# Attention's exponential images: one of four moved from VectorE to GpSimd, in three batches of four

## The chip, the core and the metric

The kernel runs on one core of one Trainium2 chip. The metric is the device time of one execution in microseconds (us). The core has five engines that run side by side and wait for each other by semaphores. The profile's names for them are PE (TensorE, matrix products into PSUM), DVE (VectorE), ACT (ScalarE), POOL (GpSimd) and SP (SyncE, which only issues DMAs here); PEld is PE's loading of weights.

## What is computed

Four layers over x of 2048 rows and 512 columns in bfloat16: a spectral layer A, an attention layer B, then both again with the same weights. Each adds its result to x.

```python
x = x + A(layernorm(x))        # rfft2, times W, irfft2
x = x + B(layernorm(x))
x = x + A(layernorm(x))
x = x + B(layernorm(x))

def B(x):                      # 32 heads of 16, one shared key and value head
    q = (x @ wq).reshape(2048, 32, 16)
    k, v = x @ wk, x @ wv
    scores = einsum("qhd,kd->hqk", q, k) * 16 ** -0.5
    return einsum("hqk,kd->qhd", softmax(scores), v).reshape(2048, 512) @ wo
```

The change lies in B, apart from one small table.

## The kernel before

**Groups and steps.** An attention layer (attention_layer, L529) works through 32 groups: 4 blocks of 512 queries times 8 sets of 4 heads. A group has 64 score tiles of 128 keys by 512 queries, 16 key chunks (kc) times 4 heads (h). Three quarters of them, those with h != kc % 4, get their exponential on ACT, three tiles at a time: one such triple is a step, so a group has 16 steps (the first group of a layer has 18, for its first four key chunks go to ACT altogether). `s0[g]` is the first step of group g.

**The other quarter goes to DVE**, as integer arithmetic. For one tile a step, `t_new` (L725) turns the scores in PSUM into 16-bit integers, steps of a logarithm. Four such tiles, from four key chunks, are a batch b (four batches a group, one per four steps). From each batch four images (L731, `s_new`, 128x2048) are made with different offsets (PH_OFF): read as bfloat16, an image is a piecewise linear exponential, and the sum of the four with weights PH_W smooths the error out. So DVE makes one t_new and one image in every step, the image one to four steps behind the last t_new of its batch.

**PE** makes the scores: `dv` (L601, one tile in a PSUM tile of its own with one buffer) for DVE and `sc` (L601, three tiles, two buffers) for ACT. It then multiplies with the values (`pv_new`, L713): four matmuls for an image and three for a triple of exponentials, all summed in one PSUM tile of the group. The values' matrix has the weights of the images in it and a column of ones, whose sum is the softmax denominator.

**The order of the work** is written out by hand. The loop at L734 walks the steps n; `chain` (L541) ties each engine's instructions to the order in which the loop issued them. In a step come, in this order: work that was put off (`later`), the eviction of a finished group, dve_step (dv, t_new, image), act_step (sc, exponential e), then pv_step with the matmuls of two steps earlier (LAG = 2). PE thus queues dv of a step, then sc, then the matmuls, and an earlier one that waits holds up the later ones.

**A group's boundary.** Two steps into the next group `evict` (L614) copies the finished sum from PSUM (`o`, L616); in the same step, in place of pv_step, PE projects the queries of the group after next (L459) into the PSUM buffer that o has left. One step later `qevict` (L462) casts them to `qt` (L464) and clears half of the rows with a bitwise AND against a table (L465). Only then can the matmuls of the new group start, for they use the same PSUM buffer; those of two steps are made together. The denominators go to DRAM and back, are inverted (L624), and are spread to all rows by DMA (`rb`, L629).

**POOL** multiplies o with rb (L657), in three cuts of 176, 176 and 160 columns in three steps (12 to 14 of the group). `pace` (L605) makes each cut wait for the latest image on DVE.

**A layer's end.** After the last step the output projection is made in PSUM triples (L767 on, `triple`), and each 128x512 result is added to x by `finish` (L682): with `with_x` PE adds x by an identity matmul and ACT casts (L685), without it DVE adds x (L687). In the first attention layer, two of a triple go to ACT and one to DVE (`n_x`, L764); statistics and normalisation of the next layer's input run between them. In the last layer all of these go to DVE, and the last four results (three in one PSUM triple, one by itself) go to ACT, except the second.

Of the kernel before, what the change touches and what calls it, by code (L numbers as in the profile page):

```python
# [10 lines left out]
ALU = mybir.AluOpType  # L11
P = 128
BF = mybir.dt.bfloat16
# [4 lines left out]
NT = 16  # L18
NC = 4
R = 4  # L20
T = 4
# [5 lines left out]
I16 = mybir.dt.int16  # L27
# [11 lines left out]
T_MUL = SCALE * LOG2E * 256.0  # L39
# [3 lines left out]
def host_tables():  # L43
    import ml_dtypes
    bf = lambda a: np.ascontiguousarray(np.asarray(a, dtype=np.float32).astype(ml_dtypes.bfloat16))
    f32 = lambda a: np.ascontiguousarray(np.asarray(a, dtype=np.float32))
    w0 = 2 * np.pi / 2048.0
    tabs = {}

    sp = (128 * np.arange(4)[None, None, :, None] + np.arange(P)[:, None, None, None]).astype(np.float64)  # L50
    tt = np.arange(4)[None, :, None, None].astype(np.float64)
    k1 = np.arange(256)[None, None, None, :].astype(np.float64)
    ang = w0 * k1 * (4 * sp + tt)
    alt = np.broadcast_to(1.0 - 2.0 * (sp % 2), ang.shape[:3] + (1,))
# [36 lines left out]
    tabs["KAB"] = f32(np.stack([1.0 - half, -THETA * half], axis=1))  # L91
    tabs["QAND"] = np.ascontiguousarray(np.broadcast_to(np.where(half == 0, -1, 0x7FFF).astype(np.int16)[:, None], (P, 512)))
    tabs["ident"] = bf(eye)
    return tabs

# [350 lines left out]
def attention_inputs(nc, tabs, shared, xn_sb, aw):  # L446
# [15 lines left out]
    def qevict(ps):  # L462
        qt = shared.tile([P, 512], BF, tag="QT", bufs=3)
        nc.vector.tensor_copy(out=qt, in_=ps)  # L464
        nc.vector.tensor_tensor(out=qt.bitcast(I16), in0=qt.bitcast(I16), in1=tabs["QAND"], op=ALU.bitwise_and)  # L465
        return qt

    def filler(psum, rhs, n):
# [60 lines left out]
def attention_layer(nc, tc, tabs, shared, lnpool, x_sb, xn_sb, aw, prep, nxt, store):  # L529
    with ExitStack() as ctx:  # L530
# [26 lines left out]
        act_tiles = []  # L557
        for g in range(NG):
            s0[g] = len(act_tiles)
            us = [(g, kc, h) for kc in range(NT) for h in range(4)  # L560
                  if h != kc % 4 or (g == 0 and kc < 4)]
            act_tiles += [us[i:i + 3] for i in range(0, len(us), 3)]
        s0[NG] = len(act_tiles)
        d_score, d_phase = {}, {}
        for g in range(NG):
            for kc in range(NT):
                if not (g == 0 and kc < 4):
                    d_score[s0[g] + kc - 4] = (g, kc)
                    if g == 0:
                        base = 4 + (kc // 4 - 1) * 4  # L570
                    else:
                        base = s0[g] + kc - kc % 4
                    d_phase[base + kc % 4] = (g, kc // 4, kc % 4)
        LAG = 2
        first_pv, last_pv = {}, {}
        pv_list = {}
        evict_at = {s0[g + 1] + LAG: g for g in range(NG)}
        qproj_at = {s0[g + 1] + LAG: g + 2 for g in range(NG - 2)}
        for n0 in range(s0[NG]):
            lst = []  # L580
            if n0 in d_phase:
                g, b, j = d_phase[n0]
                lst += [(g, 4 * b + i, i, j, n0) for i in range(4)]
            lst += [(g, kc, h, -1, n0) for (g, kc, h) in act_tiles[n0]]
            assert len({u[0] for u in lst}) == 1
            n = n0 + LAG
            if n in evict_at:
                n += 1
            pv_list.setdefault(n, []).extend(lst)
            for u in lst:  # L590
                first_pv.setdefault((u[0], u[2]), u)
                last_pv[(u[0], u[2])] = u

        psc = ctx.enter_context(tc.tile_pool(name="psc", bufs=2, space=bass.MemoryType.PSUM))
        psd = ctx.enter_context(tc.tile_pool(name="psd", bufs=1, space=bass.MemoryType.PSUM))
# [3 lines left out]
        def score(dst, g, kc, h):  # L599
            hs = slice(32 * h, 32 * h + 32)  # L600
            nc.tensor.matmul(dst, lhsT=KT[hs, kc * P:(kc + 1) * P], rhs=QT[g][hs, :], start=True, stop=True)  # L601
# [87 lines left out]
                store(r, t, nc.sync if t == T - 1 and r % 2 == 1 else nc.gpsimd)  # L689

        chain()
        def act_step(n):
# [8 lines left out]
            nc.scalar.activation(out=e[:, 0:na, :], in_=sc[:, 0:na, :], func=ACT.Exp, scale=SCALE)  # L701

        def pv_step(n):
            for u in pv_list.get(n, ()):
                g, kc, h, j, n0 = u
                if g not in pv:
                    pv_new = psp.tile([P, 512], F32, tag="pv")
                    pv[g] = pv_new
                if j < 0:
                    rhs = ex[n0][:, act_tiles[n0].index((g, kc, h)), :]  # L710
                else:
                    rhs = sb[(g, kc // 4, j)][:, h, :].bitcast(BF)
                nc.tensor.matmul(pv[g][32 * h:32 * h + 32, :], lhsT=vaug[:, max(j, 0), kc, :], rhs=rhs,  # L713
                                 start=(g > 0 and first_pv[(g, h)] == u), stop=(last_pv[(g, h)] == u),
                                 skip_group_check=True)

        def dve_step(n):
            if n in d_score:
                g, kc = d_score[n]
                dv = psd.tile([P, 512], F32, tag="dv")  # L720
                score(dv, g, kc, kc % 4)
                if kc % 4 == 0:
                    t_new = work.tile([P, 4, 512], I16, tag="T", bufs=3)
                    tb[(g, kc // 4)] = t_new
                nc.vector.tensor_scalar(out=tb[(g, kc // 4)][:, kc % 4, :], in0=dv, scalar1=T_MUL, scalar2=T_ADD,  # L725
                                        op0=ALU.mult, op1=ALU.add)
            if n in d_phase:
                g, b, j = d_phase[n]
                s_new = work.tile([P, 4, 512], I16, tag="S", bufs=7)
                sb[(g, b, j)] = s_new  # L730
                image[0] = nc.vector.tensor_scalar(out=s_new, in0=tb[(g, b)], scalar1=0.5, scalar2=16384.0 + PH_OFF[j],  # L731
                                                   op0=ALU.mult, op1=ALU.add)

        for n in range(s0[NG]):  # L734
            now[0] = n
# [25 lines left out]
            chain()  # L761


        mv, n_x = {}, 0 if nxt is None else 2  # L764

        def triple(i):
            ps = psc.tile([P, 3, 512], F32, tag="sc", name="tri")  # L767
# [249 lines left out]
```

## Time and profile before

| | us |
|---|---|
| runs | 1647.89, 1647.89, 1650.95 |
| median | 1647.89 |
| the profiled execution | 1655.24 |
| its span, first to last instruction | 1653.4 |
| first attention layer, loop of steps | 119 to 813 |
| second attention layer, loop of steps | 935 to 1630 |
| busy: PE, DVE, ACT, POOL | 1428.4, 1551.4, 1509.0, 163.2 |

The profiled execution is one run with the hardware profiler on. Its times count from the first instruction, and its span is compared with its own 1655.24, not with the median. A row of a group gives the line, the engine, the operation, what it writes and reads, shapes and count, then busy time and the mean duration of one in ns, then idle time before it and what ended that. A row of the timeline gives start and length in us; consecutive instructions of one kind may be merged into one row with a count. Neighbouring instructions of one engine overlap in the record: while DVE is never idle, a t_new of 685 ns is followed by the next operation 0.60 us after its start. The clock granted to TensorE was 0.943 over the span.

### The profile page before, as it was taken

Reading aid. Unit: us, or ns where it says so; the run is one execution under the profiler, and the core shown is the slowest. Engines: PE = TensorE matmul, PEld = TensorE weight load, DVE = VectorE, ACT = ScalarE, POOL = GpSimd, SP = SyncE. Lnnn points to the kernel's source line nnn. Section 1 sums busy time; section 2 is a strip of 40 time slices with the busy share of each in tenths; the row PEclk is TensorE's granted clock in tenths of the full one; section 3 lists DMA queues with packets and bytes.
Section 4 is the critical chain, followed back from the end, with each engine's and each line's share of the span. In section 5 each row is a group of like instructions: output and inputs, shape, how many; then the busy total and the mean of one; then the engine's idle time right before and its main releaser. Section 6 shows DMA issues by size and latency. Waiting matters only on the chain.

```text
span 1653.4 us, 32260 instructions
## 1 busy us (share of the span) xinstructions
PE 1428.4 (86%) x12768; PEld 461.3 (28%) x12768; DVE 1551.4 (94%) x2793; ACT 1509.0 (91%) x1254; POOL 163.2 (10%) x277
## 2 busy tenths in 40 slices
PE   6798888888888888888988988888888888888887
PEld 2342222222222222222333322222222222222222
DVE  6979999999999999999778799999999999999995
ACT  5369999999999999999853799999999999999994
POOL 3210000000000000000102000000000000000002
PEclk9899999999999999999998999999999999999999
DMA  8000000000000010001020000000000000000002
GB/s 289 5 1 8 17 17 17 17 16 11 16 17 17 16 30 16 16 17 30 23 71 0 1 9 16 17 17 17 17 17 17 17 17 17 12 15 17 16 17 66
DMA packets 46536, 40.78 MB, mean 25 GB/s; under 512 B 30832, under 2 KB 34416, under 8 KB 46000
## 3 DMA queue, kind: packets, MB, share of 16 engines
q1 hardware_dynamic: 45712, 36.88, 7.9%
q8 instruction: 100, 1.64, 0.4%
q0 software_dynamic: 672, 1.84, 0.3%
q14 instruction: 52, 0.43, 0.1%
HBM read 33.57 MB, written 3.15 MB: 22 GB/s over the span
## 4 chain that ended last, share of the span: by engine, by line
ACT 32%; DVE 29%; issue 21%; PE 16%; POOL 1%; DMA 1%; SPq 0%; DVEq 0%; POOLq 0%; ACTq 0%
ACT e L701 31%; DVE t_new L725 11%; DVE s_new L731 9%; PE pv_new L713 4%; PE fd L268 2%; PE dv L601 2%; DVE o L616 2%; DVE qt L464 2%; PE sc L601 2%; DVE qt L465 1%; DVE stats L125 1%; PE tri L679 1%; PE ps L391 1%; PE ps L379 1%; PE ps L192 1%
## 5 line engine op out<-in xcount | busy, mean ns | idle before, releaser
L701 ACT ACTIVATE e<-sc 128x1536 bf16<-128x1536 f32 (+1 forms) x1028 | 1387.5, 1532 | 6.2 <-PE sc L601 5.8
L725 DVE TENSOR_SCALAR t_new<-dv 128x512 int16<-128x512 f32 x1016 | 695.5, 685 | 26.4 <-PE dv L601 8.9
L731 DVE TENSOR_SCALAR s_new<-t_new 128x2048 int16<-128x2048 int16 x1016 | 698.6, 689 | 0.0
L601 PE MATMUL dv<-qt,KT 32*128 32x512 bf16 x1016 | 384.1, 378 | 108.1 <-DVE t_new L725 106.0
L601 PE MATMUL sc<-qt,KT 32*128 32x512 bf16 x3080 | 409.0, 383 | 33.9 <-ACT e L701 4.3
L713 PE MATMUL pv_new<-s_new,vaug 128*32 128x512 bf16 x4064 | 410.4, 391 | 27.2 <-DVE qt L464 27.2
L713 PE MATMUL pv_new<-e,vaug 128*32 128x512 bf16 x3080 | 412.9, 390 | 0.3 <-ACT e L701 0.3
L601 PEld LDWEIGHTS <-KT 32*128 32x128 bf16 x4096 | 201.2, 91 | 721.4 <-issue 702.8
L713 PEld LDWEIGHTS <-vaug 128*32 128x32 bf16 x7144 | 135.3, 94 | 265.7 <-issue 251.2
L657 POOL TENSOR_TENSOR ot_new<-o,rb 128x176 bf16<-128x176 f32 (+1 forms) x96 | 55.0, 575 | 700.0 <-DVE s_new L731 649.3
L657 POOL TENSOR_TENSOR od<-o,rb 128x176 bf16<-128x176 f32 (+1 forms) x90 | 49.4, 549 | 598.7 <-DVE s_new L731 598.7
L459 PE MATMUL ps<-xT,wq_sb 128*128 128x512 bf16 x256 | 67.3, 387 | 11.4 <-DVE o L616 11.4
L379 PE MATMUL ps<-tab_PS,st 128*128 128x512 bf16 x128 | 36.1, 448 | 16.2 <-DVE st L327 12.7
L385 ACT CAST U<-ps 128x512 bf16<-128x512 f32 x24 | 14.0, 585 | 36.4 <-PE ps L379 36.4
L268 PE MATMUL fd<-X,tab_DT 128*128 128x512 bf16 x192 | 43.9, 390 | 2.7 <-DVE X L242 2.7
L274 ACT CAST xn_sb<-fd 128x512 bf16<-128x512 f32 x32 | 18.7, 585 | 28.5 <-PE fd L268 28.5
L464 DVE CAST qt<-ps 128x512 bf16<-128x512 f32 x64 | 44.2, 691 | 0.4 <-PE ps L459 0.4
L616 DVE COPY o<-pv_new 128x512 f32<-128x512 f32 x64 | 43.8, 685 | 0.2 <-PE dv L601 0.2
L125 DVE BATCH_NORM_STATS2 stats<-x_sb 128x6 f32<-128x512 bf16 x46 | 30.7, 676 | 7.2 <-DMA x_sb<-in_A_x_dram 3.5
L459 PEld LDWEIGHTS <-wq_sb 128*128 128x128 bf16 x256 | 25.0, 97 | 40.2 <-issue 16.6
L391 PE MATMUL ps<-U,IT 128*128 128x512 bf16 x128 | 34.3, 390 | 0.0
L192 PE MATMUL ps<-FT,xn_sb 128*128 128x512 bf16 x80 | 22.2, 439 | 13.9 <-ACT xn_sb L134 10.9
(154 smaller groups left out, 602.1 us busy)
## 6 DMA issues: line engine op xcount, KB each, us to landing
rb<-d SPq DMA_DIRECT2D x256, 64.0 KB
FT<-const_FT SPq DMA_DIRECT2D x8, 512.0 KB
IT<-const_IT SPq DMA_DIRECT2D x8, 512.0 KB
x_sb<-in_A_x_dram SPq DMA_DIRECT2D x4, 512.0 KB
ot_new<-od SPq DMA_DIRECT2D x120, 16.0 KB
out_dram<-x_sb POOLq DMA_DIRECT2D x14, 128.0 KB, 2.2
tab_DT<-const_DT SPq DMA_DIRECT2D x1, 1280.0 KB
wr_raw<-in_A_w_r_dram SPq DMA_DIRECT2D x1, 1028.0 KB
```

The source lines that it names most:

```text
L268: nc.tensor.matmul(pss[i], lhsT=DT[:, b, w, 128 * fb:128 * fb + 128], rhs=X[:, b, part, c, :, :].rearrange("p k j -> p (k j)"), start=star ...
L379: nc.tensor.matmul(ps, lhsT=st[c][:, t, vec, q, fb, :], rhs=PS[:, fb, w, :], start=(k == 0), stop=(k == 3))
L391: nc.tensor.matmul(ps, lhsT=IT[:, t, part, c, r * P:(r + 1) * P], rhs=U[:, t, part, c, :], start=(k == 0), stop=(k == 3 and r % 2 == 1), s ...
L459: nc.tensor.matmul(ps, lhsT=wq_sb[:, c, hg, :], rhs=xTq[qb][:, c, :], start=(c == 0), stop=(c == NC - 1))
L464: nc.vector.tensor_copy(out=qt, in_=ps)
L601: nc.tensor.matmul(dst, lhsT=KT[hs, kc * P:(kc + 1) * P], rhs=QT[g][hs, :], start=True, stop=True)
L616: nc.vector.tensor_copy(out=o, in_=pv.pop(g))
L657: pace(nc.gpsimd.tensor_tensor(out=dst[:, a:b], in0=o[:, a:b], in1=rb[:, a:b], op=ALU.mult))
L701: nc.scalar.activation(out=e[:, 0:na, :], in_=sc[:, 0:na, :], func=ACT.Exp, scale=SCALE)
L713: nc.tensor.matmul(pv[g][32 * h:32 * h + 32, :], lhsT=vaug[:, max(j, 0), kc, :], rhs=rhs, start=(g > 0 and first_pv[(g, h)] == u), stop=(l ...
L725: nc.vector.tensor_scalar(out=tb[(g, kc // 4)][:, kc % 4, :], in0=dv, scalar1=T_MUL, scalar2=T_ADD, op0=ALU.mult, op1=ALU.add)
L731: image[0] = nc.vector.tensor_scalar(out=s_new, in0=tb[(g, b)], scalar1=0.5, scalar2=16384.0 + PH_OFF[j], op0=ALU.mult, op1=ALU.add)
```

## The change

On POOL, batches 0, 1 and 2 of a group (the first group of a layer has only 1 and 2) get their fourth image, in four pieces of 128x512, one piece per step at steps 4b to 4b + 3, each paced behind the latest image on DVE. DVE makes the other three images of these batches, and all four of batch 3. They lie at steps 0, 4, 5 (batch 0), 6 to 8, 9 to 11 and 12 to 15, so that steps 1, 2 and 3 have none. The matmuls are taken from a queue of lists, at most three lists a step, everything that is left in the step ahead of an eviction, and none in the step of the eviction.

```diff
-    tabs["QAND"] = np.ascontiguousarray(np.broadcast_to(np.where(half == 0, -1, 0x7FFF).astype(np.int16)[:, None], (P, 512)))
+    tabs["QAND"] = np.ascontiguousarray(np.where(half == 0, -1, 0x7FFF).astype(np.int16)[:, None])
...
-        nc.vector.tensor_tensor(out=qt.bitcast(I16), in0=qt.bitcast(I16), in1=tabs["QAND"], op=ALU.bitwise_and)
+        nc.vector.tensor_scalar(out=qt.bitcast(I16), in0=qt.bitcast(I16), scalar1=tabs["QAND"], scalar2=None, op0=ALU.bitwise_and)
...
+                for j, k in enumerate(((0, 4, 5), (6, 7, 8), (9, 10, 11), (12, 13, 14, 15))[b]):
+                    d_image[s0[g] + k] = (g, b, j)
+                if b < 3:
+                    for i in range(4):
+                        p_image[s0[g] + 4 * b + i] = (g, b, i)
...
+        queue = []
+        for n in range(s0[NG] + LAG):
+            n0 = n - LAG
+            if n0 in d_image:
+                g, b, j = d_image[n0]
+                queue.append([(g, kc, h, j, i) for i, (kc, h) in enumerate(batch[(g, b)])])
+            if n0 in p_image and p_image[n0][2] == 3:
+                g, b, _ = p_image[n0]
+                queue.append([(g, kc, h, 3, i) for i, (kc, h) in enumerate(batch[(g, b)])])
+            if 0 <= n0:
+                queue.append([(g, kc, h, -1, (n0, i)) for i, (g, kc, h) in enumerate(act_tiles[n0])])
             if n in evict_at:
-                n += 1
+                continue
+            count = len(queue) if n + 1 in evict_at else min(len(queue), 3)
+            pv_list[n] = sum(queue[:count], [])
+            queue = queue[count:]
...
+        scratch = shared.tile([P, 3, 4, 512], I16, tag="G", bufs=1)
+
+        def steps_of(g, b):
+            k = len(tb)
+            if (g, b) not in tb:
+                tb[(g, b)] = scratch[:, k % 3]
+            return tb[(g, b)]
...
         def dve_step(n):
...
+            if n in d_image:
+                g, b, j = d_image[n]
                 s_new = work.tile([P, 4, 512], I16, tag="S", bufs=7)
                 sb[(g, b, j)] = s_new
-                image[0] = nc.vector.tensor_scalar(out=s_new, in0=tb[(g, b)], scalar1=0.5, scalar2=16384.0 + PH_OFF[j],
-                                                   op0=ALU.mult, op1=ALU.add)
+                image[0] = nc.vector.tensor_scalar(out=s_new, in0=tb[(g, b)], **image_of(j))
+            if n in p_image:
+                g, b, i = p_image[n]
+                if i == 0:
+                    pool_new = work.tile([P, 4, 512], I16, tag="SP", bufs=2)
+                    sb[(g, b, 3)] = pool_new
+                pace(nc.gpsimd.tensor_scalar(out=sb[(g, b, 3)][:, i, :], in0=tb[(g, b)][:, i, :], **image_of(3)))
...
-        mv, n_x = {}, 0 if nxt is None else 2
+        mv, n_x = {}, 0 if nxt is None else 3
...
-            outproj(12 + i, pf[i], i != 1)
+            outproj(12 + i, pf[i], i < 3)
...
-            finish(12 + i, pf[i], i != 1)
+            finish(12 + i, pf[i], i < 3)
```

`image_of(j)` holds the two constants of an image, as before, and `to_steps` the t_new instruction, as before. The integer tiles were three buffers of a tag of their own and are now thirds of `scratch`, which lies in the shared buffer of tag G; that buffer holds the spectral layers' G and U, and is free between them. The AND's table shrinks from 512 columns to one. At the layers' ends, in the first attention layer all three of a triple go to ACT, and in both layers the last four go to ACT for the three of one PSUM triple and to DVE for the one by itself.

More of the change, by code (lines that the diff above doesn't have):

```diff
@@ L559, in attention_layer @@
             s0[g] = len(act_tiles)
-            us = [(g, kc, h) for kc in range(NT) for h in range(4)
-                  if h != kc % 4 or (g == 0 and kc < 4)]
+            us = [(g, kc, h) for kc in range(NT) for h in range(4) if h != kc % 4 or (g == 0 and kc < 4)]
             act_tiles += [us[i:i + 3] for i in range(0, len(us), 3)]
         s0[NG] = len(act_tiles)
-        d_score, d_phase = {}, {}
+        d_score, d_image, p_image, batch = {}, {}, {}, {}
         for g in range(NG):
[L566 to L573, printed above, removed]
+            for b in range(NT // 4):
+                if g == 0 and b == 0:
+                    continue
+                batch[(g, b)] = [(4 * b + i, i) for i in range(4)]
+                for i in range(4):
+                    d_score[s0[g] + 4 * b + i - 4] = (g, b, i)
+                for j, k in enumerate(((0, 4, 5), (6, 7, 8), (9, 10, 11), (12, 13, 14, 15))[b]):
+                    d_image[s0[g] + k] = (g, b, j)
+                if b < 3:
+                    for i in range(4):
+                        p_image[s0[g] + 4 * b + i] = (g, b, i)
@@ L574, in attention_layer @@
         LAG = 2
-        first_pv, last_pv = {}, {}
-        pv_list = {}
+        first_pv, last_pv, pv_list = {}, {}, {}
         evict_at = {s0[g + 1] + LAG: g for g in range(NG)}
         qproj_at = {s0[g + 1] + LAG: g + 2 for g in range(NG - 2)}
[L579 to L586, printed above, removed]
-            if n in evict_at:
-                n += 1
-            pv_list.setdefault(n, []).extend(lst)
-            for u in lst:
+        queue = []
@@ new lines, in attention_layer @@
+        for n in range(s0[NG] + LAG):
[8 more added lines that the diff above has]
+                queue.append([(g, kc, h, -1, (n0, i)) for i, (g, kc, h) in enumerate(act_tiles[n0])])
+            if n in evict_at:
+                continue
+            count = len(queue) if n + 1 in evict_at else min(len(queue), 3)
+            pv_list[n] = sum(queue[:count], [])
+            queue = queue[count:]
+            for u in pv_list[n]:
@@ L591, in attention_layer @@
                 first_pv.setdefault((u[0], u[2]), u)
                 last_pv[(u[0], u[2])] = u
+            assert len({u[0] for u in pv_list[n]}) <= 1
+        assert not queue
         psc = ctx.enter_context(tc.tile_pool(name="psc", bufs=2, space=bass.MemoryType.PSUM))
@@ L691, in attention_layer, with to_steps @@
         chain()
+        scratch = shared.tile([P, 3, 4, 512], I16, tag="G", bufs=1)
[4 more added lines that the diff above has]
+            return tb[(g, b)]
+        def to_steps(g, b, i, ps):
+            nc.vector.tensor_scalar(out=steps_of(g, b)[:, i, :], in0=ps, scalar1=T_MUL, scalar2=T_ADD,
+                                    op0=ALU.mult, op1=ALU.add)
         def act_step(n):
@@ L704, in pv_step @@
             for u in pv_list.get(n, ()):
-                g, kc, h, j, n0 = u
+                g, kc, h, j, k = u
                 if g not in pv:
@@ L709, in pv_step @@
                 if j < 0:
-                    rhs = ex[n0][:, act_tiles[n0].index((g, kc, h)), :]
+                    rhs = ex[k[0]][:, k[1], :]
                 else:
-                    rhs = sb[(g, kc // 4, j)][:, h, :].bitcast(BF)
+                    rhs = sb[(g, kc // 4, j)][:, k, :].bitcast(BF)
                 nc.tensor.matmul(pv[g][32 * h:32 * h + 32, :], lhsT=vaug[:, max(j, 0), kc, :], rhs=rhs,
@@ L715, in pv_step, with image_of @@
                                  skip_group_check=True)
+        def image_of(j):
+            return {"scalar1": 0.5, "scalar2": 16384.0 + PH_OFF[j], "op0": ALU.mult, "op1": ALU.add}
         def dve_step(n):
             if n in d_score:
-                g, kc = d_score[n]
+                g, b, i = d_score[n]
                 dv = psd.tile([P, 512], F32, tag="dv")
[L721 to L725, printed above, removed]
-                                        op0=ALU.mult, op1=ALU.add)
-            if n in d_phase:
-                g, b, j = d_phase[n]
+                score(dv, g, 4 * b + i, i)
+                to_steps(g, b, i, dv)
+            if n in d_image:
+                g, b, j = d_image[n]
                 s_new = work.tile([P, 4, 512], I16, tag="S", bufs=7)
                 sb[(g, b, j)] = s_new
-                image[0] = nc.vector.tensor_scalar(out=s_new, in0=tb[(g, b)], scalar1=0.5, scalar2=16384.0 + PH_OFF[j],
-                                                   op0=ALU.mult, op1=ALU.add)
+                image[0] = nc.vector.tensor_scalar(out=s_new, in0=tb[(g, b)], **image_of(j))
[5 more added lines that the diff above has]
+                pace(nc.gpsimd.tensor_scalar(out=sb[(g, b, 3)][:, i, :], in0=tb[(g, b)][:, i, :], **image_of(3)))
         for n in range(s0[NG]):
```

## The prediction

> **What bounds the kernel now.** I read the page first, then busy time by stage, then the timeline of one group boundary, engine by engine. The page's busiest groups:
>
> ```profile
> PE 1428.4 (86%) x12768; PEld 461.3 (28%) x12768; DVE 1551.4 (94%) x2793; ACT 1509.0 (91%) x1254; POOL 163.2 (10%) x277
> L701 ACT ACTIVATE e<-sc 128x1536 bf16<-128x1536 f32 (+1 forms) x1028 | 1387.5, 1532 | 6.2 <-PE sc L601 5.8
> L725 DVE TENSOR_SCALAR t_new<-dv 128x512 int16<-128x512 f32 x1016 | 695.5, 685 | 26.4 <-PE dv L601 8.9
> L731 DVE TENSOR_SCALAR s_new<-t_new 128x2048 int16<-128x2048 int16 x1016 | 698.6, 689 | 0.0
> ```
>
> DVE (VectorE) leads, and POOL (GpSimd) is nearly free, which invites a move from one to the other. The two attention layers by stage say otherwise (columns: window, stretch, then PE, PEld, DVE, ACT and POOL busy, clock, DMA):
>
> ```profile
> 119.00:813.00 694.00, 603.03 (x5747) 180.85 (x5745) 677.55 (x1138) 692.97 (x514) 52.90 (x94) 0.95 0.07 17
> 935.00:1630.00 695.00, 605.18 (x5745) 180.79 (x5745) 678.19 (x1138) 693.62 (x514) 52.22 (x93) 0.95 0.06 16
> ```
>
> There ACT (ScalarE) is never idle: 692.97 of 694.00. It makes the same 514 exponentials per layer after the change, so only ACT's lost time can be won. Recorded busy time hides some, because neighbouring exponentials overlap in the record. The timeline of ACT alone:
>
> ```profile
> 689.24 16.23 ACT L701 ACTIVATE e<-sc 128x1536 bf16<-128x1536 f32 x12
> 710.83 16.23 ACT L701 ACTIVATE e<-sc 128x1536 bf16<-128x1536 f32 x12
> ```
>
> Twelve in 16.23, of which the first takes 1.45 by itself: (16.23 - 1.45)/11 = 1.344 us a step. Sixteen would be 21.50, but the two stretches start 21.59 apart. So **0.09 us a group is lost**, once, between steps 3 and 4 of a group (steps counted from its first ACT tile). By the ends of all exponentials this happens at 29 ordinary boundaries a layer; each layer's first boundary loses about 0.62.
>
> Why there? DVE, then PE (TensorE):
>
> ```profile
> 706.08 0.68 DVE L731 TENSOR_SCALAR s_new<-t_new 128x2048 int16<-128x2048 int16 x1
> 706.68 0.69 DVE L616 COPY o<-pv_new 128x512 f32<-128x512 f32 x1
> 707.28 0.68 DVE L725 TENSOR_SCALAR t_new<-dv 128x512 int16<-128x512 f32 x1
> 707.87 0.69 DVE L731 TENSOR_SCALAR s_new<-t_new 128x2048 int16<-128x2048 int16 x1
> 708.50 0.69 DVE L464 CAST qt<-ps 128x512 bf16<-128x512 f32 x1
> 709.23 0.43 DVE L465 TENSOR_TENSOR qt<-qt,tab_QAND 128x512 int16<-128x512 int16 x1
> 709.57 0.68 DVE L725 TENSOR_SCALAR t_new<-dv 128x512 int16<-128x512 f32 x1
> ...
> 706.06 0.40 PE L713 MATMUL pv_new<-e,vaug 128*32 128x512 bf16 x3
> 707.41 1.05 PE L459 MATMUL ps<-xT,wq_sb 128*128 128x512 bf16 x4 [0.17 <-DVE o L616]
> 710.31 0.37 PE L601 MATMUL dv<-qt,KT 32*128 32x512 bf16 x1
> ```
>
> The chain: last PV matmul, eviction o, query projection, cast, AND, t_new of step 3, then dv and sc of step 4 at 710.31, just behind that t_new's end at 710.25 (PE queues dv ahead of sc). The exponential of step 4 starts 1.26 after the start of t_new 3. When DVE is well ahead, the same distance is 2.4; below 1.26 ACT waits. That is the slack I count with.
>
> **The change, part by part.**
>
> *Images off DVE.* Three of 16 images a group go (one DVE operation starts 0.60 after the other, so 3 x 0.60 = 1.8 us of DVE), and steps 1 to 3 have none. Over the group that is worth nothing, since ACT sets the step. In the chain, o no longer waits behind the image of 706.08: the last PV ends at 706.46, 0.06 later (as dv after t_new) is 706.52 instead of 706.68. o 0.69, 0.04 to the projection, 1.05, 0.04 to the cast give 708.34 (the image of 707.87 would have held it until 708.47, and is gone too). The AND comes 0.73 later, at 709.07. As a tensor_scalar with a per-partition operand it is like L480's 128x512 (404 ns, next start after 0.32) instead of 426 ns and 0.34: t_new at 709.39, 0.18 earlier. Needed is 0.09. What is late next: the PV matmuls of step 3. They are 14 now (709.25 to about 710.31) and 10 after, since steps 1 to 3 make fewer lists; at 0.08 each (7 take 0.56 in a plain step) they end near 709.9 and don't hold dv. The 58 ordinary boundaries give 58 x 0.09 = **-5.2 us**. The two first boundaries I take at nothing (bounds 0 and -1.2), since DVE starts a layer with little lead.
>
> *Pieces on POOL.* Each group adds twelve tensor_scalar of 128x512 int16, at steps 0 to 11, each sent after that step's image by `pace`. Those of steps 0 to 3 run back to back behind one image while DVE has none; their cost is nothing if they are done by the AND: 4 x 0.77 from 705.50 ends at 708.6, before 709.07. Those of steps 4 to 11 meet the next image. How the two engines meet shows at one product:
>
> ```profile
> 742.28 0.56 POOL L657 TENSOR_TENSOR od<-o,rb 128x176 bf16<-128x176 f32 x1 [18.69 <-DVE s_new L731]
> 742.66 0.73 DVE L731 TENSOR_SCALAR s_new<-t_new 128x2048 int16<-128x2048 int16 x1
> ```
>
> The product ends 0.18 after the image's start, and the image takes 0.73 instead of its usual 0.685; the other products end 0.12 into an image and cost it nothing. So an image waits for POOL's end, less 0.13. A piece starts 0.08 after an image's end (as the products do), and the next image begins 0.52 after it when DVE runs at its own pace of 1.20 a step. A piece of p us therefore delays the image by 0.08 + p - 0.52 - 0.13 = p - 0.57. DVE's step becomes 0.63 + p, against ACT's 1.344: **below p = 0.71 the piece is hidden**; above it DVE sets the pace.
>
> The Trainium skill's page "SBUF — State Buffer" (Who interferes with whom) says that VectorE's two-port modes and GpSimd exclude each other, the second one waiting the whole time. The trace agrees (0.73 against 0.68), and by that rule this change can lose outright.
>
> What is p? The trace has no such operation on int16. The nearest are:
>
> ```profile
> L136 POOL TENSOR_SCALAR xn_sb<-x_sb,rstd,nb 128x512 bf16<-128x512 bf16 x22 | 16.8, 768 | 90.0 <-DVE nb L131 74.1 <-DVE mv L126 10.6 <-ACT xT L493 5.2
> L657 POOL TENSOR_TENSOR od<-o,rb 128x176 bf16<-128x176 f32 x60 | 33.6, 561 | 579.4 <-DVE s_new L731 579.4
> ```
>
> Bounds: 0.22 (a free-running 128x4 tensor_scalar, L364: launch alone) and 1.27 (128x512 with two inputs, L651). L136 has the piece's size and one input but two per-partition operands, which the piece lacks. On DVE such operands cost 0.125: with them 512 and 1536 columns take 404 and 674 ns, so 2048 would take 0.81, and the image without them takes 0.685. I take L136 less that: p = 0.645. DVE's step is then 1.28, under 1.344: cost nothing, with 0.065 to spare. Without the deduction p is 0.77, and that is the first rival.
>
> The Trainium skill's "GPSIMD Engine Reference" (3.1) gives one-input bodies of up to two operations 1.03 cycles an element, and loops of best case 1.8. As an estimate, 512 x 1.03 at its 1.2 GHz plus the launch row is 0.66, and the sum stays -5.8; with 1.8 it is 0.77 before the launch, the rival's case.
>
> *PV order.* The same matmuls; 11 instead of 7 at steps 5, 9 and 13 (+0.32). PE sits 0.4 a step between dv and sc waiting for ACT, which covers it.
>
> *Storage.* The steps tile becomes thirds of one buffer, each rewritten 12 steps later, long after its readers. The zeroing of G at a layer's end (809.42) waits a little longer for the last image; G is first written at 832.92. Smaller QAND load: beside the start's other loads. All nothing.
>
> *Layer ends.* The last four evictions go ACT, DVE, ACT, ACT now, and ACT waits 0.76 for DVE on the same PSUM triple:
>
> ```profile
> 1648.06 0.69 DVE L687 TENSOR_TENSOR x_sb<-three,x_sb 128x512 bf16<-128x512 f32 x1 [4.91 <-ACT x_sb L685]
> 1648.78 0.58 ACT L685 CAST x_sb<-three 128x512 bf16<-128x512 f32 x1 [0.76 <-DVE x_sb L687]
> ```
>
> After: ACT's three from 1647.44 at 0.48 spacing end at 1649.0, DVE's one beside them, instead of 1649.85. The stores behind keep some of it: **-0.6 us** (0 to -0.9). At layer one's end four more identity matmuls (4 x 0.22 on a busy PE, +0.9) stand against the same 0.76 wait there: nothing (+0.9 to -0.8).
>
> *Sum:* -5.2 - 0.6 = -5.8. It is made in the profiled execution (span 1653.4, with what lies around it 1655.24); the runs shown have a median of 1647.89, 0.4% less, and I set the difference against that: **1642.1 us** (for this case alone 1638.5 to 1645).
>
> **Rivals.** *Pieces of 0.77 slow DVE.* Its step is then 1.40 at steps 4 to 11, of which one is hidden by the reciprocal: 7 x 0.055 = 0.38 us, against 0.3 of slack at step 5, so ACT loses 0.1 there. Only five free steps (12 to 0) gain back 0.14 each, so DVE reaches the boundary with 0.5 of slack, not 1.1; o starts about 0.35 late and the boundary loses 0.2 to 0.3. Together 0.3 to 0.4 for the 0.09 of now: 60 x 0.25 = +15, less 0.6: about 1660. It decides from p = 0.74 on; each 0.01 more costs 8 x 0.01 x 60 = 5 us. For it: L136's row as it stands. Against: the operands.
>
> *What is saved is spent.* p near 0.74, or some other wait of the boundary (o, the projection, the cast) takes 0.09 again: only the ends remain, 1647.
>
> *Far slower pieces.* Int16 at the two-input price (1.27): 8 x (1.90 - 1.344) = 4.4 us a group, some 1920. Or the thirds are tracked as one tile, each t_new waits for the piece before it, and the pieces aren't parallel at all: over 1900 too. Converted types already run on POOL at ordinary rates, and slices of one tile are used by several engines at once (xn_sb), so little.
>
> **Chances.** Forecast 0.50, pieces near 0.77 0.28, spent 0.12, far slower 0.10. The range takes forecast, spent and the first rival: 1638.5 to 1662. A measurement tells 0.2% (3.3 us) from no change: faster 0.48, same 0.15, slower 0.37.
>
> **What would show it.** The duration of the pieces; images at 685 ns (hidden) or longer at steps 5 to 12; 1.344 from step 3 to 4 in place of 1.44; ACT's waits before the first rival's steps 10 to 13; the final casts without DVE between. The forecast falls if pieces last over 0.71, or if o, the cast or t_new of step 3 isn't earlier.

## The result and the profile after

The changed kernel takes **1641.22 us** (median of 4 runs, 1639.79 to 1641.93), the kernel before 1649.31 on the same chip (4 runs, 1647.89 to 1650.95). The ratio is 0.995 with a 95% interval of 0.9932 to 0.9967: 8.1 us, or 0.5%, faster. The profiled execution took 1640.85, with a span of 1639.1.

One caution first. The profiled execution of before ran at a mean TensorE clock of 0.943, that of after at 0.994, so the 14.3 us between their spans hold more than the change. (The clock here is the share of full speed that the profile records as granted to TensorE.) For the attention loops a run of the kernel before with other layer ends (e2 below, clock 0.994) serves as a better "before".

The groups of the page of after that answer to those shown of before:

```profile
PE 1383.7 (84%) x12772; PEld 480.1 (29%) x12772; DVE 1475.0 (90%) x2599; ACT 1503.5 (92%) x1258; POOL 647.5 (40%) x1037
L723 ACT ACTIVATE e<-sc 128x1536 bf16<-128x1536 f32 (+1 forms) x1028 | 1380.4, 1694 | 4.5 <-PE sc L611 4.3
L758 POOL TENSOR_SCALAR pool_new<-scratch 128x512 int16<-128x512 int16 x760 | 464.1, 619 | 770.3 <-DVE s_new L752 690.6
L752 DVE TENSOR_SCALAR s_new<-scratch 128x2048 int16<-128x2048 int16 x826 | 611.7, 742 | 0.0
```

A piece on POOL lasts 0.619 us (0.645 was chosen). The 826 images left on DVE now last 742 ns in the mean, 689 before: 190 fewer images, 86.9 us less busy time on DVE, although 190 x 0.689 would be 131. The other 44 us came back inside the images' own durations, as waiting for POOL: without the pieces (e9 below) an image lasts 684 ns.

The first layer's loop as a stage (window, stretch, PE, PEld, DVE, ACT and POOL busy, clock, DMA); in the second ACT is busy for 686.92 of 689.00:

```profile
119.00:805.00 686.00, 581.23 (x5719) 189.79 (x5720) 639.94 (x1042) 685.65 (x512) 293.50 (x473) 1.00 0.06 17
```

ACT is as full as it was; busy time still cannot show whether it loses anything. The timeline of ACT over two boundaries of layer one can:

```profile
688.64 45.92 ACT L723 ACTIVATE e<-sc 128x1536 bf16<-128x1536 f32 x34
```

The first of the 34 takes 1.59 by itself, so a step is (45.92 - 1.59)/33 = 1.343. That is the undisturbed step of before, now with the boundaries in it.

The boundary, DVE and then POOL. It is another group than the one shown of before, so read the distances, not the times:

```profile
379.61 0.69 DVE L626 COPY o<-pv_new 128x512 f32<-128x512 f32 x1 [0.27 <-PE pv_new L735]
380.22 0.68 DVE L711 TENSOR_SCALAR scratch<-dv 128x512 int16<-128x512 f32 x1
381.42 0.69 DVE L464 CAST qt<-ps 128x512 bf16<-128x512 f32 x1 [0.52 <-PE ps L459]
382.14 0.35 DVE L465 TENSOR_SCALAR qt<-qt,tab_QAND 128x512 int16<-128x512 int16 x1
382.41 0.68 DVE L711 TENSOR_SCALAR scratch<-dv 128x512 int16<-128x512 f32 x1
...
378.81 2.36 POOL L758 TENSOR_SCALAR pool_new<-scratch 128x512 int16<-128x512 int16 x4 [3.21 <-DVE s_new L752]
```

DVE now waits for PE twice, 0.27 for the last PV matmul and 0.52 for the projection: no image stands before o or the cast. The AND lasts 0.35, not 0.43, and t_new of step 3 (scratch, 382.41) starts 2.19 after that of step 2; before it was 2.29, and 2.27 in e2 at the higher clock. The four pieces are done at 381.17, 0.97 ahead of the AND. The next sections turn on that gap.

**Where the time went, by stage.** "Lost" is what a stretch between the ends of its exponentials has over 1.3435 us a step, the distance of two ends in the steps that nothing holds up, without the first steps of a layer (0.6 to 0.75 in every kernel). "Between" runs from the end of layer one's last exponential to the end of layer two's first, "tail" from the end of layer two's last to the end of the span.

| kernel (clock) | lost, first boundaries of layers 1 + 2 | lost, other steps of layers 1, 2 | between | tail |
|---|---|---|---|---|
| before (0.943) | 0.64 + 0.77 | 2.84, 3.14 + 0.94 | 123.1 | 22.9 |
| e2, before with the new ends (0.994) | 0.59 + 0.58 | 1.74, 1.99 | 119.7 | 22.1 |
| after (0.994) | 0.04 + 0.03 | 0.03, -0.08 | 119.7 | 21.8 |

The 0.94 is lost in layer two alone, at every 64th step; its cause is open. An ordinary boundary costs 2.84/29 = 0.098 us at the lower clock and 1.74/29 = 0.060 at the higher one. The change takes both kinds of boundary away: at equal clock 3.8 at the ordinary and 1.1 at the first ones, 4.9 in all.

**Where in the chain.** Recorded starts of exponentials drift against their ends (in the undisturbed steps 1.330 apart, ends 1.3435), so the chain is measured from ends (medians of the 60 boundaries of a trace, us):

| kernel | o starts before the end of step 1's exponential | t_new of step 3 starts before the end of step 3's |
|---|---|---|
| e2, before with the new ends | 1.48 | 1.30 |
| e3, before with the short AND | 1.48 | 1.37 |
| e5, after with the old AND | 1.65 | 1.46 |
| after | 1.65 | 1.54 |

The change brings o forward by 0.17 and shortens the way from there to t_new by 0.07.

### The profile page after: what moved, and what is told of

The parts are those of the page before. It is cut to its first block, busy times and chain, and to the rows that moved or that the text cites. A ratio compares the mean times of both kernels' runs of the same rounds, so it can differ in the third digit from the quotient of the medians.

```text
span 1639.1 us, 33712 instructions
## 1 busy us (share of the span) xinstructions
PE 1383.7 (84%) x12772; PEld 480.1 (29%) x12772; DVE 1475.0 (90%) x2599; ACT 1503.5 (92%) x1258; POOL 647.5 (40%) x1037
## 4 chain that ended last, share of the span: by engine, by line
DVE 37%; ACT 29%; PE 20%; issue 13%; POOL 1%; DMA 1%; SPq 0%; POOLq 0%; ACTq 0%; DVEq 0%
ACT e L723 27%; DVE scratch L711 18%; DVE s_new L752 11%; PE ps L459 4%; PE dv L611 3%; DVE qt L464 3%; PE pv_new L735 2%; PE sc L611 2%; PE fd L268 2%; PE ps L192 1%; PE tri L689 1%; PE ps L391 1%; DVE stats L125 1%; PE ps L379 1%; DVE den L634 1%
## 5 line engine op out<-in xcount | busy, mean ns | idle before, releaser
L758 POOL TENSOR_SCALAR pool_new<-scratch 128x512 int16<-128x512 int16 x760 | 464.1, 619 | 770.3 <-DVE s_new L752 690.6
L711 DVE TENSOR_SCALAR scratch<-dv 128x512 int16<-128x512 f32 x1016 | 687.8, 677 | 45.8 <-PE sc L611 33.3
L752 DVE TENSOR_SCALAR s_new<-scratch 128x2048 int16<-128x2048 int16 x826 | 611.7, 742 | 0.0
L611 PEld LDWEIGHTS <-KT 32*128 32x128 bf16 x4096 | 218.8, 91 | 695.3 <-issue 656.6
L735 PE MATMUL pv_new<-e,vaug 128*32 128x512 bf16 x3080 | 389.7, 380 | 0.4 <-ACT e L723 0.4
L735 PE MATMUL pv_new<-s_new,vaug 128*32 128x512 bf16 x3304 | 330.1, 389 | 27.2 <-DVE qt L464 27.2
L735 PE MATMUL pv_new<-pool_new,vaug 128*32 128x512 bf16 x760 | 74.5, 383 | 0.0
L667 POOL TENSOR_TENSOR ot_new<-o,rb 128x176 bf16<-128x176 f32 (+1 forms) x96 | 66.8, 709 | 18.9 <-DVE s_new L752 18.9
L667 POOL TENSOR_TENSOR od<-o,rb 128x176 bf16<-128x176 f32 (+1 forms) x90 | 61.0, 691 | 18.9 <-DVE s_new L752 18.9
L136 POOL TENSOR_SCALAR xn_sb<-x_sb,rstd,nb 128x512 bf16<-128x512 bf16 x22 | 16.8, 767 | 86.4 <-DVE nb L131 76.4
```

Of the source, the lines that this page charges most:

```text
L667: pace(nc.gpsimd.tensor_tensor(out=dst[:, a:b], in0=o[:, a:b], in1=rb[:, a:b], op=ALU.mult))
L711: nc.vector.tensor_scalar(out=steps_of(g, b)[:, i, :], in0=ps, scalar1=T_MUL, scalar2=T_ADD, op0=ALU.mult, op1=ALU.add)
L758: pace(nc.gpsimd.tensor_scalar(out=sb[(g, b, 3)][:, i, :], in0=tb[(g, b)][:, i, :], **image_of(3)))
```

## The experiments

Each ratio is to the kernel before on the same chip. "Step k" counts from a group's first ACT tile.

**e1, the layer ends undone** in the changed kernel:

```
-        mv, n_x = {}, 0 if nxt is None else 3
+        mv, n_x = {}, 0 if nxt is None else 2
-            outproj(12 + i, pf[i], i < 3)
+            outproj(12 + i, pf[i], i != 1)
-            finish(12 + i, pf[i], i < 3)
+            finish(12 + i, pf[i], i != 1)
```

> The changed kernel with the layers' ends as they were before. Theory A (placement: the 0.09 us that ACT lost at every group's boundary is gone because o, cast, AND and t_new of step 3 no longer stand behind images, and the ends give some tenths of a us): 1641.8, 7.5 us under before, and ACT's last casts again interrupted by DVE. Theory B (relief: DVE has three images a group fewer, wherever they stood): the same. Theory C (the difference is the granted clock, 0.94 in the profile of before and 0.99 after): no part of the change has a stable effect, so within 2 us of either kernel by chance, and ACT's loss at the boundary follows the clock of the run.

Measured: 1642.58, ratio 0.9962 (0.9949 to 0.9975), 2.0 above after by the ratios ((0.9962 - 0.995) x 1649), with intervals that overlap. In the profiles the tail is 22.5 against 21.8, and the loops are equal within 0.1. The time between, 121.2 against 119.7, settles nothing: e3, which has the old ends too, has 118.6.

**e2, the layer ends alone**, put into the kernel before (the same three lines the other way):

> The kernel before with the new ends alone. A and B: 0.6 us under before (0 to 0.9), ACT still loses 0.09 at each boundary. C: nothing.

Measured: 1647.71, ratio 0.9995 (0.9986 to 1.0005): not to be told from none by its time. By the ratios the ends are worth 0.8 here and 2.0 in e1, and the rest of the change has most of the gain.

**e3, the shorter AND alone**, in the kernel before:

```
-    tabs["QAND"] = np.ascontiguousarray(np.broadcast_to(np.where(half == 0, -1, 0x7FFF).astype(np.int16)[:, None], (P, 512)))
+    tabs["QAND"] = np.ascontiguousarray(np.where(half == 0, -1, 0x7FFF).astype(np.int16)[:, None])
-        nc.vector.tensor_tensor(out=qt.bitcast(I16), in0=qt.bitcast(I16), in1=tabs["QAND"], op=ALU.bitwise_and)
+        nc.vector.tensor_scalar(out=qt.bitcast(I16), in0=qt.bitcast(I16), scalar1=tabs["QAND"], scalar2=None, op0=ALU.bitwise_and)
```

> The kernel before with the AND alone as a tensor_scalar with one operand a partition (353 ns in the changed kernel's profile, 426 before). t_new of step 3 then starts 0.07 earlier. A, if t_new of step 3 is what holds dv of step 4: 58 x 0.07 = 4 us under before. A, if the 14 PV matmuls of step 3 hold it just as well: 0 to 1 us under before. B and C: nothing.

Measured: 1644.81, ratio 0.9974 (0.9963 to 0.9985), 4.4 us: half of the change's gain from one instruction a group.

```profile
L465 DVE TENSOR_SCALAR qt<-qt,tab_QAND 128x512 int16<-128x512 int16 x64 | 22.4, 353 | 2.1
```

t_new of step 3 starts 2.19 after that of step 2 in place of e2's 2.27, and the other steps lose -0.08 and 0.62 a layer. PE still has 14 PV matmuls in step 3, so these were not what holds dv. The first boundaries still lose 0.52 and 0.65, and layer two its 0.91 at every 64th step.

**e5, the old AND** (two full operands, 426 ns) in the changed kernel, the same lines the other way:

> The changed kernel with the AND of before (two inputs, a table of 512 columns). The AND alone gave 4.4 us on the kernel before (e3). Theory A (placement: images out of steps 1 to 3): t_new of step 3 comes 0.07 later than in the changed kernel, but o and the cast still come 0.1 earlier than before, and 10 or 11 PV matmuls stand where 14 stood: 1641 to 1642.5, at most 1 us over the changed kernel, ACT's loss at the ordinary boundaries under 0.02. Theory D (the AND is what does it, the moved images do little): 1645 to 1646, 0.06 lost at each boundary as with the new ends alone (e2).

Measured: 1642.23, ratio 0.9952 (0.994 to 0.9963), 0.3 us above after by the ratios. The ordinary steps lose 0.03 and 0.07 a layer, the first boundaries 0.10 each. So the new place of the images, with the order of the PV matmuls that goes with it, suffices too. **Either half lifts the ordinary boundaries, and the gains don't add**: 0.06 to 0.10 was needed, the AND gives 0.07, the place 0.17, and both together 0.24. Only the placement cures the first boundaries.

**e4, sixteen images on DVE** in the thirteen steps, no pieces; three steps make two images:

```
-                for j, k in enumerate(((0, 4, 5), (6, 7, 8), (9, 10, 11), (12, 13, 14, 15))[b]):
-                    d_image[s0[g] + k] = (g, b, j)
-                if b < 3:
-                    for i in range(4):
-                        p_image[s0[g] + 4 * b + i] = (g, b, i)
+                for j, k in enumerate(((0, 4, 4, 5), (6, 7, 8, 8), (9, 10, 11, 12), (12, 13, 14, 15))[b]):
+                    d_image.setdefault(s0[g] + k, []).append((g, b, j))
...
```

> The changed kernel without POOL's pieces: DVE makes all 16 images of a group, none in steps 1 to 3, two in steps 4, 8 and 12. DVE's work is 32 x 0.60 + o 0.60 + cast 0.73 + AND 0.27 + reciprocal 0.16 = 20.96 us a group, against ACT's 21.50. A: placement is enough, 5 to 8 us under before. B: no relief, no gain, and slower by some us where two images in one step hold up dv (a step of 1.8 against 1.344). C: nothing.

Measured: 1686.54, ratio 1.0228 (1.0213 to 1.0243), 37 us slower than before. The theory that the place of the images is enough by itself fell. DVE and ACT behind a boundary:

```profile
393.73 0.69 DVE L707 TENSOR_SCALAR scratch<-dv 128x512 int16<-128x512 f32 x1 [0.46 <-PE sc L607]
394.34 1.28 DVE L747 TENSOR_SCALAR s_new<-scratch 128x2048 int16<-128x2048 int16 x2
395.54 0.69 DVE L707 TENSOR_SCALAR scratch<-dv 128x512 int16<-128x512 f32 x1
...
396.80 6.95 ACT L719 ACTIVATE e<-sc 128x1536 bf16<-128x1536 f32 x5 [0.17 <-PE sc L607]
```

Step 4 has two images, and the next t_new comes 1.81 later (395.54 - 393.73) instead of 1.20. DVE comes out of the boundary without lead, so ACT waits two steps later (0.17), and again two steps behind the other double steps. Four steps with five images take 1.81 + 3 x 1.20 = 5.41, ACT's four take 5.374: the lead doesn't come back. The steps lose 23.1 and 20.9 a layer, first boundaries included. To free three steps, three images must leave DVE; it is for this that the pieces are on POOL.

**e7, no pieces, first attempt.** The fourth image is left out and an image of the batch that DVE makes is read again:

```
-                    rhs = sb[(g, kc // 4, j)][:, k, :].bitcast(BF)
+                    rhs = sb[(g, kc // 4, 2 if j == 3 and kc < 12 else j)][:, k, :].bitcast(BF)
...
-                pace(nc.gpsimd.tensor_scalar(out=sb[(g, b, 3)][:, i, :], in0=tb[(g, b)][:, i, :], **image_of(3)))
```

> The changed kernel without POOL's pieces: the fourth image of batches 0 to 2 is left out, and the third stands in for it in the PV matmuls. A (pieces of 0.62 are hidden): images back from 730 to 685 ns, DVE further ahead of ACT, and the time the same, within 1 us of the changed kernel. Rival (the pieces still cost ACT something at steps 4 to 11): 2 to 6 us under it.

Measured: 1706.15, ratio 1.0335 (1.0321 to 1.035). Neither theory had this. The experiment was at fault: in the first batch the image read again is made in step 5, the very step whose matmuls use it (the other two batches have a step or two to spare). From PE's waits (instruction and what it waits for; us in total, times, longest):

```profile
PE pv_new L735 <- DVE s_new L752: 86.2, 62, 1.4
```

After has no such wait in its list. The 62 waits are one a group, all in step 5: PE stood up to 1.4 us at a matmul, with sc of the next step behind it.

**e9, no pieces, second attempt**, with the batch's first image read again (`0 if j == 3 and kc < 12 else j`), which is made at step 0, 6 or 9:

> The changed kernel without GpSimd's 12 pieces a group; where TensorE would read the fourth image of a batch it reads the first again, which is made at step 0, 6 or 9 and is long there, so this leaves out a quarter of the images of three batches in four, 30 us of VectorE's or 464 us of GpSimd's work, and keeps every matmul. It is the one run of the study that must separate the pieces from all else. Theory (the pieces cost nothing as long as VectorE's lead lasts): images 685 ns at all steps in place of 730 to 965, the exponentials' stretches 689 us as in the changed kernel, time within 1.5 us of it (1640 to 1643). Rival (the pieces' lengthening of the images still holds ScalarE somewhere): 1 to 4 us shorter, seen as a loss of the rest below that of the changed kernel. If the earlier run without pieces was long for its stand-in alone, its 31 us per layer are gone.

Measured: 1639.62, ratio 0.9949 (0.9937 to 0.9961); after has 0.995. Images last 684 ns, and the steps lose 0.03 and 0.72 a layer, after's 0.03 and -0.08. **The pieces cost nothing that these runs can tell** (the two intervals allow some 3 us either way), and e7's 31 us a layer were its stand-in.

**e8, longer pieces**: their two constants as per-partition operands, as L136 has them:

```
+        offs = shared.tile([P, 2], F32, tag="offs", bufs=1)
+        nc.gpsimd.memset(offs[:, 0:1], 0.5)
+        nc.gpsimd.memset(offs[:, 1:2], 16384.0 + PH_OFF[3])
...
-                pace(nc.gpsimd.tensor_scalar(out=sb[(g, b, 3)][:, i, :], in0=tb[(g, b)][:, i, :], **image_of(3)))
+                pace(nc.gpsimd.tensor_scalar(out=sb[(g, b, 3)][:, i, :], in0=tb[(g, b)][:, i, :], scalar1=offs[:, 0:1],
+                                             scalar2=offs[:, 1:2], op0=ALU.mult, op1=ALU.add))
```

> The changed kernel with the pieces' two constants taken from a 128x2 tile, one operand a partition each, as L136 takes its own. By the prediction's deduction the pieces last 0.62 + 0.125 to 0.15 = 0.74 to 0.77; the images behind them 685 + (p - 0.57) = 0.86 to 0.89; DVE's step is 1.37 to 1.40 at steps 4 to 11, over ACT's 1.344, and the time is that of the first rival, 1652 to 1662, with ACT losing at steps 10 to 13 and at the boundary. If the operands cost POOL nothing: 0.62, and 1641.

Measured: 1696.15, ratio 1.0274 (1.026 to 1.0288), 55 us over after. The pieces, and DVE's timeline in steps 8 and 9 of a group:

```profile
L762 POOL TENSOR_SCALAR pool_new<-scratch,offs 128x512 int16<-128x512 int16 x760 | 584.6, 774 | 707.8 <-DVE s_new L756 457.3 <-PE pv_new L735 226.6 <-DVE scratch L711 23.9
...
401.41 0.67 DVE L711 TENSOR_SCALAR scratch<-dv 128x512 int16<-128x512 f32 x1
402.00 0.90 DVE L756 TENSOR_SCALAR s_new<-scratch 128x2048 int16<-128x2048 int16 x1
402.82 0.67 DVE L711 TENSOR_SCALAR scratch<-dv 128x512 int16<-128x512 f32 x1
```

The operands cost 0.774 - 0.619 = 0.155 us a piece. Images last 0.90 and DVE's step is 1.41 (402.82 - 401.41), where the prediction's 0.63 + p gives 1.404. So this is the first rival as it was described, but a group loses some 0.86 us (25.3 and 26.1 over 30 groups of each layer), where the rival had 0.3 to 0.4.

**e6, images at steps 1 and 2** in the changed kernel:

```
-                for j, k in enumerate(((0, 4, 5), (6, 7, 8), (9, 10, 11), (12, 13, 14, 15))[b]):
+                for j, k in enumerate(((0, 1, 2), (4, 5, 6), (8, 9, 10), (12, 13, 14, 15))[b]):
```

> The changed kernel with DVE's 13 images at steps 0, 1, 2, 4, 5, 6, 8, 9, 10 and 12 to 15: o and the cast stand behind images again as before, POOL's pieces and the short AND stay. A: the part that the placement adds to the AND is lost, 1643 to 1645 as e3 (first boundary of a layer loses its 0.5 again). D: 1641, the placement is worth nothing. Theory B (relief of DVE wherever): 1641.

Measured: 1672.49, ratio 1.0133 (1.0118 to 1.0148), 31 us over after and far beyond what was expected. DVE and POOL at a boundary:

```profile
388.56 0.79 DVE L465 TENSOR_SCALAR qt<-qt,tab_QAND 128x512 int16<-128x512 int16 x1
389.27 0.67 DVE L711 TENSOR_SCALAR scratch<-dv 128x512 int16<-128x512 f32 x1
...
388.00 1.20 POOL L758 TENSOR_SCALAR pool_new<-scratch 128x512 int16<-128x512 int16 x2 [1.18 <-DVE s_new L752]
```

With images at steps 1 and 2 the pieces are paced up to the boundary. The third still runs for 0.06 when the AND starts, the fourth starts 0.02 behind the AND's start (388.58) and ends at 389.20; the AND lasts until 389.35, 0.79 instead of 0.35. t_new of step 3 comes 2.63 after that of step 2, and ACT loses 0.50 a boundary. The Trainium skill's page "SBUF — State Buffer" (Who interferes with whom) has VectorE's two-port forms and GpSimd exclude each other. The AND agrees with it: it ends 0.15 behind the fourth piece. Two runs test the reading.

**e10: e6 with every piece from the fourth on one step later**, so that none is issued at step 3:

```
-                        p_image[s0[g] + 4 * b + i] = (g, b, i)
+                        p_image[s0[g] + 4 * b + i + (4 * b + i > 2)] = (g, b, i)
```

> The run with images at steps 0, 1, 2 (31 us longer than the change), with one thing more: the fourth piece of a group's first batch, and all later ones, one step later, so that no piece is issued at step 3 beside the AND. Theory (that run lost its time because the piece beside the AND stretched it from 353 to 759 ns): the AND is 353 ns again, dv of step 3 starts 2.2 us after that of step 2 in place of 2.63, and nearly all of the 31 us come back: 1641 to 1647. Rival (an image at steps 1 and 2 takes VectorE's lead before the boundary, whatever the AND does): the AND is short and the time stays within 8 us of 1672.

Measured: 1659.64 (1652.27 to 1672.76), ratio 1.0071 (1.0042 to 1.0099). The AND is 353 ns again and t_new of step 3 comes 2.18 after that of step 2, as expected; but only 13 of the 31 us came back. (Its median run has a clock of 0.985, e6's have 0.991 to 0.993; its one run at 0.992 took 1652.27, so 13 is the low end.) The steps still lose 5.89 and 7.09 a layer, 0.2 a boundary, and the first boundaries 1.65 and 0.69, some 15 in its trace where e6's loses 32. Its trace gives the rest. The image of step 1 stands before o and, beside a piece, lasts 0.76: o starts 1.32 before the end of step 1's exponential, in e2 1.48, in after 1.65. The image of step 2 stands before the cast. So both theories hold a part, by the traces about half each: the AND beside a piece, and the missing free steps.

**e11: e6 with the old AND** (lines as in e5):

> The run with images at steps 0, 1, 2, with one thing more: the AND with its two full operands as before the change (426 ns alone). Theory A (only the form with one operand of 512 waits for or is held by a piece beside it): the AND takes 426 to 450 ns beside a piece, most of the 31 us come back, 1645 to 1655. Theory B (either form is held by a piece that runs beside it): the AND takes 750 to 850 ns and the time stays at 1668 to 1680.

Measured: 1650.91, ratio 1.0013 (1.0003 to 1.0023); 22 of the 31 us came back, as theory A had it. DVE and POOL:

```profile
384.97 0.42 DVE L465 TENSOR_TENSOR qt<-qt,tab_QAND 128x512 int16<-128x512 int16 x1
...
384.41 1.46 POOL L758 TENSOR_SCALAR pool_new<-scratch 128x512 int16<-128x512 int16 x2 [1.18 <-DVE s_new L752]
```

The AND with two full operands takes its usual 0.42, and here **the piece waits**: the two pieces take 1.46 together instead of 1.20. With such neighbours the slower form is the better one. e10 and e11 also answer theory B, relief of DVE wherever it comes from: both take three images a group from DVE without freeing steps 1 and 2, and neither is faster than the kernel before.

## Why the prediction was right, point by point

The forecast case is what happened: 1642.1 forecast, 1641.22 measured. That the two are 0.9 apart is in part luck. The forecast was a gain of 5.8 on a median of 1647.89; the measured gain is 8.1 (5.4 to 11.2) on 1649.31, and two terms of the sum were off in opposite directions.

- *ACT bounds, 1.344 a step.* Shown: 34 exponentials over two boundaries at 1.343.
- *0.09 a boundary, -5.2.* Right in kind. The loss is 0.098 in the trace at 0.943 and 0.060 in e2's at 0.994; the query projection in the chain lasts 1.05 in the one and 1.02 in the other, which is most of the difference. So at the clock of the ordinary runs the term is 3.8. What made up for it is the next point, and that was luck.
- *The two first boundaries, taken at nothing with a bound of -1.2.* Mis-sized: they gave 1.1, almost the bound. DVE starts a layer with little lead, as said, but o and the cast wait for PE now, so that the lead isn't what the boundary needs: there o starts 1.43 before the end of step 1's exponential, 0.95 in e2.
- *o, projection, cast.* As worked out: each starts when PE is done, 0.27 and 0.52 after DVE's last work. With the AND, t_new of step 3 was to come 0.18 earlier; against the ends it comes 0.24 earlier than in e2 (0.17 for o, 0.07 for the AND).
- *AND 0.02 shorter.* Mis-sized: 0.07 shorter in duration (426 to 353 ns). The row it was taken from (L480) has two operands for each partition, the AND has one. By e3 this alone nearly closes the ordinary boundaries.
- *PV matmuls of step 3, 14 to 10.* The step is not needed: with 14 of them in e3, the ordinary boundaries of layer one lose nothing.
- *p = 0.645.* Measured 0.619: L136 less a price for its operands was the right row, and e8 puts that price at 0.155 where 0.125 was taken. The 0.125 was DVE's price, lent to POOL on no evidence from POOL; that it came so near is luck.
- *An image is delayed by p - 0.57.* For 0.619 that is 0.05: images behind a piece last 730 ns, and 685 + 45 is what the formula says. Twice a group they last about 803, behind the first piece of a batch, which starts 0.16 behind the image before it instead of 0.08 (at step 8 the trace names the piece's buffer as what it waits for, PE pv_new, 60 times in all; at step 4 it names nothing but the image); once about 965, beside the products of 128x176. These were not foreseen, and the lead paid for them: e9, without pieces, is no faster. An image waits less than it overlaps, as the formula has it: 0.18 of overlap costs 0.045, 0.26 costs 0.12.
- *Layer ends.* ACT's final three are together now, as said, and end 1.56 after the first starts instead of 2.41:

```profile
1633.67 1.56 ACT L695 CAST x_sb<-three 128x512 bf16<-128x512 f32 x3 [16.43 <-PE three L689]
```

  Of these 0.85 the stores behind keep 0.28 (from the last cast to the end of the span 3.85 instead of 3.57), so -0.6 at the end as forecast, and every trace with the old ends has the old figures, every other the new 1.56. Between the layers the runs tell no gain or loss from the 2 us by which that stretch varies.
- *The first rival, 1660 with pieces of 0.77.* Its mechanism is real, and its price was three times too small: e8 is 47 us over before where the rival had 14, and at 1696 it lies above the top of the range. The step that failed is "ACT loses 0.1 there". At 1.41 a step, and 1.49 behind the first piece of a batch, DVE has no lead left at step 9, and ACT loses 0.5 in steps 9 to 15. The boundary came out nearer: o starts 0.36 later than in e2, as the rival had it, and 0.35 is lost there, where it had 0.2 to 0.3. The range held because p was right, not because it covered p's bounds.

Measured terms at equal clock: 3.8 + 1.1 at the boundaries and 0.8 to 2.0 at the ends, 5.7 to 6.9; 0.9 more if before keeps, at the higher clock, the loss at every 64th step that e3 still shows there. The medians differ by 8.1, with an interval of 5.4 to 11.2: agreement within what the timing can tell.

Open: layer two's 0.9 at every 64th step in before and in e3, absent in e2 and after; why e10's first boundary of layer one lost 1.65; and what the new order of the PV matmuls is worth by itself, since no run has it alone.

## What to carry to other kernels

When one engine is full and another runs ahead of it, look for the places where the lead is used up: a few hundredths of a microsecond on the chain of a group's boundary are worth more here than 87 us of busy time. Work moved to GpSimd is free only as long as what it adds to VectorE's instructions beside it is less than VectorE's lead: compare a piece's length with the gap between those instructions first, and price what happens beyond it with the lead gone at the next bottleneck, not with the excess alone. And before a short instruction of a critical chain is made shorter, see what runs beside it.

## What the runs showed of the hardware

- One operation, two forms, two losers: beside a 128x512 piece on POOL the bitwise AND as a tensor_scalar lasted 787 ns (353 alone, e6; the mean of 759 over all 64, which the expectation of e10 has, includes four that met no piece), while as a tensor_tensor it kept its 426 and a piece took 879 (617 alone, e11).
- On POOL two per-partition operands raise a 128x512 int16 tensor_scalar from 0.619 to 0.774 us (e8).
- Time moves with the granted clock though TensorE is not the bound: 1652.27 at 0.992, 1659.64 at 0.985 and 1672.76 at 0.974 in e10, some 1.1 us for each 0.001; 1647.69 at 0.994 and 1654.82 at 0.987 in before, 1.0; 1639.79 at 0.994 and 1641.93 at 0.990 in after, about half of that. Only one run of a kernel has a trace, so that it is the boundaries that differ between these runs is not shown.
